# Working out the scales of staged expert weights only in slots behind a measuring pass

## The chip, the core and the metric

The kernel runs on one core of a Trainium2 chip: TensorE (PE) multiplies matrices, VectorE (DVE), ScalarE (ACT) and GpSimd (POOL) work elementwise, SyncE (SP) issues most transfers, and 16 DMA engines move the data. The metric is the time of one execution on the device, in microseconds (us); lower is better.

## What is computed

The reference is an attention layer whose output goes through a layer of experts. The attention part (a pooled softmax attention plus a narrow local one over 8 batches, 8 heads, 576 positions, 64 wide) is not touched. Behind it each of 4608 rows goes to one of eight experts:

```python
N, D, E, F = (4608, 512, 8, 1024)
expert_idx = np.argmax(logits, axis=1)
gate_w = probs[np.arange(N), expert_idx]
for e in range(E):
    mask = expert_idx == e
    h = np.maximum(x[mask] @ w1[e], 0.0)
    out[mask] = gate_w[mask, None] * (h @ w2[e])
```

## The kernel before

The attention comes first (about 350 us). Its rows are sorted into **slots** of 128 rows that share an expert. Three slots run early; then `run_slots` runs 38 more, b = 0 to 37, each as one pass of a loop that is written out in full. The slots stand in the order of their experts, so the expert changes in seven of the 38.

Products are made exact enough by splitting each operand into two float16 halves: a high one and a remainder. A slot is therefore two blocks of 24 matmuls: **mm1** (`x @ w1`, lines 1079 to 1081) and **mm2** (lines 1104 to 1106). A pass runs mm1 of its own slot and then mm2 of the slot before, so that the relu and its transposes have time. The rows x and the hidden rows h are turned by DMA transposes (tiles `xT`, line 1033, made two passes ahead; `hT`, line 1092).

An expert's weights come from HBM as float32 into a staging tile (`st`, one for w1, one for w2), 2 MB each. Before they are split they are scaled by a power of two that follows from the sum of squares of the whole matrix. That takes three steps, spread over passes:

- `measure` (lines 897 and 752): one ScalarE pass over the staged matrix, which leaves partial sums of squares in `wsq`;
- `rescale` (line 891): `total` adds them over the partitions with a tiny matmul on TensorE (line 760, columns for w1 and w2) and VectorE takes its result (line 761); `scales` makes `winv` and `wscl` in three more VectorE instructions (lines 768 and 770);
- `split_all` (lines 776 and 777): ScalarE and VectorE write the two halves of the new expert's weights. `stage_next` then issues the load of the next expert's matrix on SP, which takes place only if a flag says so.

What a pass does with the weights is decided on the chip by a **code** for each slot: 0 nothing, 1 measure w1, 2 measure w2, 3 to 5 a new expert (split; with 4 or 5 measure on the spot). `flags` loads it into a register of ScalarE, VectorE and GpSimd two slots ahead, and `renew` branches on it with `tc.If`: `renew(0, b + 1)` for w1 behind mm1, `renew(1, b)` for w2 behind mm2. Measuring comes in the second and third slot behind a new one, so the codes run: new, 0, 1, 2, then 0 until the next new one. `rescale` has no branch: it runs in 37 passes, whatever the code.

The order of work on each engine is the order in which the code is written (a manual schedule). In a pass: `flags(b + 2)`, mm1, its relu, `rescale`, `renew(0, b + 1)`, `stage_next(0, ...)`, gathers and norms, `x_split(q + 2)`, mm2 of the slot before, its output, `renew(1, b)`, `stage_next(1, ...)`, gate and store. An engine that passes an untaken `tc.If` takes an event instead, which waits until the engine's own earlier work is finished and then adds what the body would have added to the engine's count.

Of the kernel before, what the change touches and what calls it, by code (L numbers as in the profile page):

```python
# [15 lines left out]
ET = mybir.EngineType  # L16
# [32 lines left out]
class Kern:  # L49
# [834 lines left out]

    def flags(self, b):
        nc, f = self.nc, self.flg[:1, b, :]
        code = nc.values_load(f[:, 2:3], engines=(ET.Activation, ET.DVE, ET.Pool), min_val=0, max_val=5)
        self.ft[b] = [code, nc.sync.value_load(f[:, 0:1], min_val=0, max_val=1),
                      nc.sync.value_load(f[:, 1:2], min_val=0, max_val=E - 1)]

    def rescale(self):

        self.total(slice(0, 2))
        self.scales(slice(0, 2))

    def measure(self, which):
        self.square(self.st[which], which, None)
# [36 lines left out]
    def run_slots(self, q0, q1):  # L934

        last = q1 - 1
        for q in range(q0, q1):
            b = q - NEARLY
            if b + 2 < q1 - NEARLY:
                self.flags(b + 2)  # L940
            self.mm1(q)
            if not b:
                self.mm2_part(q - 1, 6, ps=self.begun)
            if q < last:
                self.rescale()
                self.renew(0, b + 1)
                self.stage_next(0, b + 1)
            if not b:
                self.out_rows(q - 1, self.begun)
                self.store(q - 1)  # L950
            if q + 4 < q1:
                self.gather(q + 4)
            if q < last:
                self.norms(q + 1)
            if q + 2 < q1:
                self.x_size(q + 2)
            self.logits(q)
            if q + 2 < q1:
                self.x_split(q + 2)
            if q > q0:  # L960
                ps = self.mm2_part(q - 1)
                if q < last:
                    self.out_rows(q - 1, ps)
            if q > q0:
                self.renew(1, b)
                if q == last:
                    self.out_rows(q - 1, ps)
                self.stage_next(1, b)
            self.gate(q)
            if q > q0:  # L970
                self.store(q - 1)
            self.scale_gate(q)
        self.mm2(last)
        self.store(last)
# [7 lines left out]
    def last_slots(self):  # L982

        q0, q1 = NEARLY + NFIX, NEARLY + NSLOT
        more = self.nc.values_load(self.flg[:1, NFIX, 3:4], min_val=0, max_val=1)  # L985
        with self.tc.If(more > 0):
            for q in range(q0, min(q0 + 4, q1)):
                self.gather(q)
            for b in (NFIX, NFIX + 1):
                self.flags(b)  # L990
            for w in range(2):
                self.renew(w, NFIX)
                self.stage_next(w, NFIX)
            self.open_slots(q0)
            self.run_slots(q0, q1)
# [125 lines left out]
    def run(self):  # L1121
# [53 lines left out]
        self.out_rows(0, ps)  # L1175
        flags = self.slot_flags()
        next(flags)
        self.hidden(2, 0, self.mm1_half(2, 0))
        for _ in range(2):
            next(w1)  # L1180
        next(flags)
        self.store(0)
        self.hidden(2, 1, self.mm1_half(2, 1))
# [59 lines left out]
```

## Time and profile before

| | us |
|---|---|
| time, median of 3 runs | 829.72 (828.9 to 831.03) |
| the profiled execution, its own time | 827.14 |
| its span in the trace | 825.4 |
| TensorE busy in the span | 732.9 (89%) |
| the stretch of the 38 slots, 382.9 to 811.6 | 428.7 |
| TensorE busy in that stretch | 404.4 |

Busy time of TensorE is the modelled length of its matmuls, which overlap: one counts 0.38 us, but the next starts 0.215 us later. So in the slots the starts are read, not the ends. "PEq" or "ACTq" stands for an engine's sequencer, which handles branches, events and register loads ("PEldq" is TensorE's).

### The profile page before, as it was taken

Reading aid. Unit: us, or ns where it says so; the run is one execution under the profiler, and the core shown is the slowest. Engines: PE = TensorE matmul, PEld = TensorE weight load, DVE = VectorE, ACT = ScalarE, POOL = GpSimd, SP = SyncE. Lnnn points to the kernel's source line nnn. Section 1 sums busy time; section 2 is a strip of 40 time slices with the busy share of each in tenths; the row PEclk is TensorE's granted clock in tenths of the full one; section 3 lists DMA queues with packets and bytes.
Section 4 is the critical chain, followed back from the end, with each engine's and each line's share of the span. In section 5 each row is a group of like instructions: output and inputs, shape, how many; then the busy total and the mean of one; then the engine's idle time right before and its main releaser. Section 6 shows DMA issues by size and latency. Waiting matters only on the chain. (4 is left out here: it accounts for less than half of the span.)

```text
span 825.4 us, 22041 instructions
## 1 busy us (share of the span) xinstructions
PE 732.9 (89%) x7460; PEld 440.6 (53%) x7460; DVE 517.5 (63%) x1571; ACT 504.1 (61%) x1095; POOL 414.8 (50%) x845
## 2 busy tenths in 40 slices
PE   7699698888797999879899989999998999998993
PEld 5487587677676777434344434444444444443441
DVE  7579598877599799773734735555463356446420
ACT  6478687777787685325654655666675347546520
POOL 6276466465557475463745344555445535544421
PEclk8889698988699889989999999999999999999997
DMA  7447856575756566764996797969598659659840
GB/s 173 114 129 169 225 122 179 135 211 131 215 134 181 137 172 222 214 140 98 199 209 133 207 180 205 220 181 228 136 278 135 142 137 259 147 117 259 140 100 21
DMA packets 246420, 138.91 MB, mean 168 GB/s; under 512 B 176626, under 2 KB 222706, under 8 KB 246272
## 3 DMA queue, kind: packets, MB, share of 16 engines
q1 hardware_dynamic: 238464, 116.05, 60.2%
q0 software_dynamic: 6560, 19.03, 8.8%
q10 hardware_dynamic: 1248, 2.11, 0.7%
q8 instruction: 61, 1.00, 0.5%
q14 instruction: 87, 0.71, 0.3%
HBM read 213.05 MB, written 20.33 MB: 283 GB/s over the span
## 5 line engine op out<-in xcount | busy, mean ns | idle before, releaser
L1079 PE MATMUL bank<-w1h,xT 128*128 128x512 f16 x328 | 126.4, 385 | 17.3 <-DMA xT<-x 16.7
L351 ACT ACTIVATE kq<-bank 64x288 f32<-64x288 f32 x256 | 109.7, 429 | 40.7 <-PE bank L347 28.3
L1104 PE MATMUL bank<-w2h,hT 128*128 128x512 f16 x328 | 126.3, 385 | 8.4 <-DMA hT<-h 8.4
L1080 PE MATMUL bank<-w1l,xT 128*128 128x512 f16 x328 | 126.0, 384 | 1.3 <-DVEq L924 1.3
L1105 PE MATMUL bank<-w2l,hT 128*128 128x512 f16 x328 | 126.3, 385 | 0.0
L1106 PE MATMUL bank<-w2h,hT 128*128 128x512 f16 x328 | 126.2, 385 | 0.0
L1081 PE MATMUL bank<-w1h,xT 128*128 128x512 f16 x328 | 126.2, 385 | 0.0
L1117 POOL DMA_INDIRECT out_dram<-o,ids x41 | 46.5, 1134 | 143.3 <-ACTq L919 110.4
L1089 DVE SCALAR_TENSOR_TENSOR h<-bank,h 128x512 f16<-128x512 f32 x82 | 55.2, 690 | 95.8 <-ACT h L1088 68.5
L1088 ACT ACTIVATE h<-bank 128x512 f16<-128x512 f32 x82 | 47.7, 594 | 98.1 <-PE bank L1081 61.6
L378 POOL TENSOR_TENSOR pool_v<-ld_v 72x256 f32<-72x256 f32 x64 | 51.1, 816 | 76.6 <-DMA ld_v<-in_v_dram 75.2
L752 ACT ACTIVATE junk<-st 128x1024 bf16<-128x1024 f32 (+1 forms) x30 | 67.6, 2252 | 5.9 <-DVE ge L669 4.8
L365 POOL TENSOR_TENSOR pool_kq<-kq 128x288 f32<-128x288 f32 x62 | 42.3, 691 | 50.8 <-ACT kq L351 45.6
L1001 POOL DMA_INDIRECT xg<-xd,ids x41 | 45.5, 1109 | 43.8 <-POOLq L925 15.6
L1079 PEld LDWEIGHTS <-xT 128*128 128x128 f16 x328 | 32.5, 99 | 59.6 <-DMA xT<-x 21.5
L477 PE MATMUL bank<-aT,vw 70*64 70x64 f32 x1152 | 46.5, 235 | 20.0 <-DMA vw<-in_v_dram 13.7
L1104 PEld LDWEIGHTS <-hT 128*128 128x128 f16 x328 | 35.0, 107 | 44.3 <-DMA hT<-h 8.8
L1049 ACT ACTIVATE lg<-lg,lmx 128x8 f32<-128x8 f32 x41 | 12.3, 301 | 72.4 <-DVE lmx L1047 72.4
L1031 DVE SCALAR_TENSOR_TENSOR x<-xg,sc,x 128x512 f16<-128x512 f32 x41 | 30.8, 751 | 40.3 <-ACT x L1028 40.2
L477 PEld LDWEIGHTS bank<-aT,vw 70*64 70x64 f32 x1152 | 41.4, 145 | 26.9 <-DMA vw<-in_v_dram 15.3
L1081 PEld LDWEIGHTS <-xT 128*128 128x128 f16 x328 | 32.4, 99 | 41.4 <-issue 3.7
L67 POOL TENSOR_SCALAR nw_t<-nw_y,nw_a 128x1 f32<-128x1 f32 x120 | 48.1, 400 | 12.1
(223 smaller groups left out, 1605.3 us busy)
## 6 DMA issues: line engine op xcount, KB each, us to landing
st<-in_moe_w_dram SPq DMA_DIRECT2D x148, 1024.0 KB
ld_k<-in_k_dram SPq DMA_DIRECT2D x64, 144.0 KB
ld_q<-in_q_dram SPq DMA_DIRECT2D x64, 144.0 KB
ld_v<-in_v_dram SPq DMA_DIRECT2D x64, 144.0 KB
xd<-xr SPq DMA_DIRECT2D x8, 1040.0 KB
vw<-in_v_dram SPq DMA_DIRECT2D x64, 122.5 KB
st<-in_moe_w_dram SPq DMA_DIRECT2D x12, 512.0 KB
vw<-in_v_dram SPq DMA_DIRECT2D x32, 67.0 KB
```

The costliest lines, as they stand in the source:

```text
L67: g.tensor_scalar(out=t, in0=y, scalar1=y, scalar2=a, op0=ALU.mult, op1=ALU.mult)
L351: nc.scalar.activation(out=kq[h * D:(h + 1) * D, w, 3 + r:3 + r + S:2], in_=ps[r * D:(r + 1) * D], func=AF.Copy)
L378: g.tensor_tensor(out=t6[:, c], in0=vr[:, :, 0:2 * D], in1=vr[:, :, 2 * D:], op=ALU.add)
L477: nc.tensor.matmul(out=ps[h * D:(h + 1) * D, (g - g0) * 64:(g - g0 + 1) * 64], lhsT=s["vw"][:, g, j + h], rhs=s["aT"][:, g, :, h], start=T ...
L752: self.nc.scalar.activation(out=junk, in_=src, func=AF.Square, accum_out=acc)
L1079: nc.tensor.matmul(out=ps, lhsT=xT[:, 0, k], rhs=self.w1h[:, k, ns], start=(k == 0), stop=False)
L1080: nc.tensor.matmul(out=ps, lhsT=xT[:, 0, k], rhs=self.w1l[:, k, ns], start=False, stop=False)
L1081: nc.tensor.matmul(out=ps, lhsT=xT[:, 1, k], rhs=self.w1h[:, k, ns], start=False, stop=(k == self.KC - 1))
L1089: nc.vector.scalar_tensor_tensor(out=h2[:, 1], in0=ps, scalar=0.0, in1=h2[:, 0], op0=ALU.max, op1=ALU.subtract)
L1104: nc.tensor.matmul(out=ps, lhsT=hh, rhs=self.w2h[:, j, :], start=(j == 0), stop=False)
L1105: nc.tensor.matmul(out=ps, lhsT=hh, rhs=self.w2l[:, j, :], start=False, stop=False)
L1106: nc.tensor.matmul(out=ps, lhsT=hl, rhs=self.w2h[:, j, :], start=False, stop=(j == self.FC - 1))
```

## The change

The code is loaded into a register of TensorE too (`flags`). `rescale_new(b)` takes the place of `rescale` in the loop: in slot 0 it is `rescale` as before, in the others `rescale` stands in two branches and runs for codes 1 and 2 only. `last_slots`, a part that only runs when more than 38 slots are needed, gets a `rescale` of its own.

```diff
     def flags(self, b):
-        code = nc.values_load(f[:, 2:3], engines=(ET.Activation, ET.DVE, ET.Pool), min_val=0, max_val=5)
+        code = nc.values_load(f[:, 2:3], engines=(ET.Activation, ET.DVE, ET.Pool, ET.PE), min_val=0, max_val=5)
...
+    def rescale_new(self, b):
+
+        if not b:
+            return self.rescale()
+        code = self.ft[b][0]
+        with self.tc.If(code > 0):
+            with self.tc.If(code < 3):
+                self.rescale()
...
             if q < last:
-                self.rescale()
+                self.rescale_new(b)
                 self.renew(0, b + 1)
...
             for b in (NFIX, NFIX + 1):
                 self.flags(b)
+            self.rescale()
             for w in range(2):
```

A branch is taken by every engine that holds the register, so TensorE now also walks through the branches of both `renew` calls, in which it has nothing to do. Line numbers behind the new function are ten higher than before (933 for 924, 928 for 919, 1091 for 1081, 1114 for 1104). TensorE's order where mm1 ends and mm2 begins, before, in slot 21 (`Activation_49`, `DMAHW7_49`, `PE_49` are the counts of ScalarE, of a DMA queue, of TensorE itself):

```order
L1080 MATMUL bank<-w1l,xT_10669 128x512
L1081 LDWEIGHTS xT_10669
L1081 MATMUL bank<-w1h,xT_10669 128x512
L760 MATMUL bank<-wsq,onesf 128x2 [waits Activation_49]
L1104 LDWEIGHTS hT [waits DMAHW7_49]
L1104 MATMUL bank<-w2h,hT 128x512 [waits Activation_49]
```

The same place now, up to the branches of `renew(0, b + 1)`, of which the first three stand here:

```order
L1091 MATMUL bank<-w1h,xT_10728 128x512
L901 COMPARE_AND_BRANCH
L902 COMPARE_AND_BRANCH
L760 MATMUL bank<-wsq,onesf 128x2 [waits Activation_49]
L902 UNCONDITIONAL_BRANCH
L902 UNCONDITIONAL_BRANCH [waits PE_49]
L901 UNCONDITIONAL_BRANCH [waits PE_49]
L933 COMPARE_AND_BRANCH
L934 COMPARE_AND_BRANCH
```

The tiny matmul stands behind two branches. In the two bodies without it an event waits for TensorE's own count (shown at the branch behind it: `[waits PE_49]`). Behind that come the branches of `renew`, and only then mm2's first weight load.

TensorE's order where mm2 ends and the next mm1 begins, before:

```order
L1106 LDWEIGHTS hT
L1106 MATMUL bank<-w2h,hT 128x512
L924 UNCONDITIONAL_BRANCH
L1079 LDWEIGHTS xT_10855 [waits DMAHW3_49]
L1079 MATMUL bank<-w1h,xT_10855 128x512 [waits Activation_49]
L1080 LDWEIGHTS xT_10855
```

Now:

```order
L1116 MATMUL bank<-w2h,hT 128x512
L928 COMPARE_AND_BRANCH
L929 COMPARE_AND_BRANCH
L929 UNCONDITIONAL_BRANCH x2
L928 UNCONDITIONAL_BRANCH x2
L1089 LDWEIGHTS xT_10917 [waits DMAHW3_49]
L887 TENSOR_LOAD flg
L1089 MATMUL bank<-w1h,xT_10917 128x512 [waits Activation_49]
```

Two branches of `renew(1, b)` come in, and behind mm1's first weight load, which waits for `xT`, the register load of the code stands ahead of mm1's first matmul.

## Rows read from the trace of the kernel before

**Rows 1.** stretches: us, busy us (count) by engine, granted clock, DMA share, GB/s

```profile
382.90:811.60 428.70, 404.42 (x1875) 185.06 (x1873) 217.63 (x664) 240.96 (x382) 200.68 (x480) 0.98 0.80 178
578.90:581.80 2.90, 2.86 (x7) 1.04 (x8) 1.86 (x6) 2.70 (x3) 2.15 (x9) 0.50 0.89 277
513.90:517.40 3.50, 1.80 (x10) 0.62 (x8) 1.65 (x2) 3.09 (x4) 1.91 (x6) 1.00 1.17 278
```

**Rows 2.** TensorE's group: count | busy us, mean ns | idle before, releaser

```profile
L760 PE MATMUL bank<-wsq,onesf 128*128 128x2 f32 x74 | 11.1, 219 | 4.0 <-ACTq L919 4.0
```

**Rows 3.** timeline (start, length in us): ordinary slot, mm1 to mm2

```profile
565.21 0.38 PE L1081 MATMUL bank<-w1h,xT 128*128 128x512 f16 x1
565.43 0.28 PE L760 MATMUL bank<-wsq,onesf 128*128 128x2 f32 x2
565.57 0.38 PE L1104 MATMUL bank<-w2h,hT 128*128 128x512 f16 x1
```

**Rows 4.** timeline: TensorE and VectorE in a slot that takes a new expert

```profile
601.01 0.38 PE L1081 MATMUL bank<-w1h,xT 128*128 128x512 f16 x1
601.89 0.39 PE L760 MATMUL bank<-wsq,onesf 128*128 128x2 f32 x2 [0.51 <-ACTq L919]
602.14 0.38 PE L1104 MATMUL bank<-w2h,hT 128*128 128x512 f16 x1
602.17 0.21 DVE L1055 TENSOR_SCALAR lsm<-lsm,sc 128x1 f32<-128x1 f32 x1 [0.16 <-DVEq L919]
```

**Rows 5.** what TensorE waited for, slots: us, times, longest

```profile
PE bank L1079 <- DMA xT<-x: 10.0, 6, 2.9
PE bank L1104 <- DMA hT<-h: 8.4, 5, 2.7
```

**Rows 6.** timeline: TensorE's matmuls that waited for a transposed matrix

```profile
410.06 0.39 PE L1079 MATMUL bank<-w1h,xT 128*128 128x512 f16 x1 [2.89 <-DMA xT<-x]
...
428.25 0.39 PE L1104 MATMUL bank<-w2h,hT 128*128 128x512 f16 x1 [0.53 <-DMA hT<-h]
...
516.08 0.39 PE L1079 MATMUL bank<-w1h,xT 128*128 128x512 f16 x1 [1.70 <-DMA xT<-x]
...
532.81 0.39 PE L1104 MATMUL bank<-w2h,hT 128*128 128x512 f16 x1 [0.77 <-DMA hT<-h]
...
578.94 0.61 PE L1104 MATMUL bank<-w2h,hT 128*128 128x512 f16 x1 [2.74 <-DMA hT<-h]
...
625.89 0.39 PE L1104 MATMUL bank<-w2h,hT 128*128 128x512 f16 x1 [2.11 <-DMA hT<-h]
...
753.88 0.39 PE L1079 MATMUL bank<-w1h,xT 128*128 128x512 f16 x1 [1.92 <-DMA xT<-x]
```

**Rows 7.** single lines: count, ns min/median/max; who waited, us, times

```profile
L924 ACTq COMPARE_BRANCH  x37: 44/44/50, 382.5 to 790.8; - x37
...
  ACT junk L1019: 2.4, 14
...
  POOL xg L1001: 17.4, 13
  DVE lg L1020: 6.9, 12
...
L752 ACT ACTIVATE junk<-st x30: 1041/1082/3617, 82.4 to 770.4; 128x1024 bf16<-128x1024 f32 x16, 128x4096 bf16<-128x4096 f32 x14
```

**Rows 8.** a matmul's start, and ScalarE's that waited for that matmul

```profile
587.92 0.38 PE L1081 MATMUL bank<-w1h,xT 128*128 128x512 f16 x1
...
588.34 0.60 ACT L1088 ACTIVATE h<-bank 128x512 f16<-128x512 f32 x1 [0.93 <-PE bank L1081]
```

**Rows 9.** register load, TensorE's branch (ns min/median/max; first, last us); its last matmul

```profile
L887 ACTq TENSOR_LOAD <-flg x37: 273/278/692, 381.0 to 777.7; - x37
...
L986 PEldq COMPARE_BRANCH  x1: 3552/3552/3552, 808.7 to 808.7; - x1
...
811.20 0.38 PE L1106 MATMUL bank<-w2h,hT 128*128 128x512 f16 x1
```

## The prediction

> **What bounds the kernel now.** I read the busy times by stretch first, then what TensorE waited for, then single slots in the timeline. In the 428.7 us of the slots TensorE counts 404.4 us of busy time at a mean granted clock of 0.98 [rows 1]; the other engines stay under 241 us. So a slot costs what its 48 matmuls and TensorE's gaps cost, and the change has to be priced at TensorE's gaps. There are three kinds. *The seam* between mm1 and mm2, where the tiny matmul of `rescale` stands: in an ordinary slot the last mm1 matmul starts at 565.21, the tiny pair at 565.43, the first mm2 matmul at 565.57 [rows 3]. The seam is 0.36 us from start to start; without the pair it would be one matmul's pace, 0.215. *The seam of a new slot* is longer, 601.01 to 602.14 [rows 4]: the tiny matmul waits for ScalarE's event at the end of the slot before. That holds 7 times, 4.0 us in all [rows 2]. *Waits for transposes*: six for `xT` (10.0 us) and five for `hT` (8.4 us) [rows 5]. The `xT` waits come at the start of mm1 one slot behind a new one; the `hT` waits at the seam one slot later. Both are ends of transfers that stand behind the loads of weights: the DMA share is near or over 1 there [rows 1].
>
> **How often.** The first branch of `renew` was decided 37 times, and 14 passes over a whole matrix ran [rows 7]. So of the 36 slots in which the new branch stands (b = 1 to 36; 37 has no `rescale`), 14 keep it and 22 skip it. The skips are the 7 new slots, the 7 behind them, and 8 more with code 0: four just ahead of a new slot, four elsewhere.
>
> **What goes.** 22 tiny pairs at 0.143 us (0.36 less 0.215): 3.1 us. The 4.0 us of waiting in new slots doesn't go with them: mm2's own first matmul waits for ScalarE's count too (the order shows `[waits Activation_49]` on it), and the split of w2 that it reads belongs to the same branch that ended late. At 602.17 VectorE's next work had just come out of its own event there [rows 4]. So mm2 could start at about 601.9 instead of 602.14: I take 0.2 us for each new slot, not 0.9. VectorE's four short instructions run beside TensorE and are worth nothing by themselves.
>
> **What comes: the stop at the seam.** In a skipped slot TensorE's event waits until all of mm1 is finished, and the branches of `renew` follow it. Nothing can be queued behind it, so mm2's first weight load, all 24 matmuls and, through them, ScalarE's output copy wait. Before, the array never ran dry here. The price isn't in the trace for TensorE, but its parts have near rows. A matmul that starts at 587.92 lets ScalarE start at 588.34: 0.42 us from start to notice [rows 8]. What such an event costs an engine that passes it and one branch is 0.17 us of idling on ScalarE (2.4 over 14) [rows 7]. With two or three branches it is 0.58 us on VectorE (6.9 over 12) and 1.34 on GpSimd (17.4 over 13) [rows 7]. So if the next slot has code 0 (one branch) the seam is at least 0.42 + 0.17 = 0.59 and at most 0.42 + 0.58 = 1.00; I take 0.76, nearer to the low end, because the branch that sends ScalarE on is 44 ns [rows 7]: net **+0.40** (0.23 to 0.64). If the next slot is new or measures (three branches), it is 0.75 to 1.76; I take 1.01, next to VectorE's row: net **+0.65** (0.4 to 1.4).
>
> By the Trainium skill, "Advanced Engine Details and Errata", section Control Flow Timing, a compare-and-branch takes about 108 ns and a plain branch 51; the rows show 44 ns for the former on ScalarE. With the page's figures (an estimate) the nets would be +0.34 and +0.60, close to mine.
>
> **What comes: a register load on TensorE** in each slot, and two branches of `renew(1, b)`. ScalarE takes 0.28 us for its own, 0.69 at most [rows 9]. TensorE's sequencer runs ahead of the array: its only branch is recorded at 808.7, while the last matmul ahead of it starts at 811.20 [rows 9]. So these are hidden behind queued matmuls, except where the queue is empty: behind the `xT` waits the load stands between the weight load that waits and the first matmul. I take **+0.35** there (0.28 to 0.69), 7 times.
>
> **What of this lies on the path.** A stop is paid only if no transfer's end comes later.
> - Four skips far from a new slot (23, 24, 30, 36): nothing waits behind them. 4 x 0.40 = +1.6.
> - Slots ahead of a new slot and the new slot itself: `xT` two passes on was made before, so its wait swallows them. But the split of w2, and with it the load that delays `hT`, starts after mm2 of the new pass. Where an `hT` wait follows, in the first five groups, lateness there remains: +0.65 - 0.2 in the first two groups, -0.2 in the next three (their slot ahead measures and keeps `rescale`): +0.3.
> - The slot behind a new one: 0.35 + 0.65 = 1.0 each, 7 times. Five times the `hT` wait follows: 0.53, about 2.2, 0.77, 2.74 and 2.11 us [rows 6], the second by difference from the total [rows 5]. It swallows all but 0.5 and 0.2: +0.7. In the last two groups no `hT` wait follows: +2.0.
>
> Sum: 1.6 + 0.3 + 0.7 + 2.0 = **+4.6 us**; the saved pairs are already in the nets.
>
> **The clock.** Four waits are followed by some 3.4 us at a granted clock of 0.5, the 1.2 GHz level, where eight matmuls start 0.43 us apart instead of 0.215: 1.7 us each. One of these stretches stands in rows 1. They follow waits of 2.11 us and more; after 1.70 and 1.92 the clock stayed at 1.00 [rows 6, 1]. Three of the four are `hT` waits (2.2, 2.74, 2.11), which come down by about 1.0 to 1.2, 1.7 and 1.1, below the longest that had no fall: -5.1. The `xT` wait of 1.70 grows by 0.2 + 0.35 to 2.25, above the shortest that had one: +1.7. Net **-3.4**, the least certain term.
>
> 4.6 - 3.4 = +1.2 us on the profiled 827.14: 828.3. The three runs' median, 829.72, lies 2.6 us above that execution, of which the kernel's waits for transfers are the natural cause; on it the forecast is **830.9**, inside 0.3% (2.5 us), about what a measurement of this kernel can tell from no change.
>
> **The rivals.**
> - *The stop is dearer* (slower). TensorE's sequencer needs for its event and branches what GpSimd's row says rather than ScalarE's: nets +0.64 and +1.4. Then the four free skips give 2.6, the last two groups 3.5, the first two 2 x 1.2, less 0.6, and the `hT` waits of 0.53 and 0.77 leave 2.2: +10.1, with the clock's -3.4 +6.7, without it +10.1: 836.4 to 839.8. It decides from nets of about 0.6 and 1.0 on, or, with my nets, if only one of the falls of the clock goes. For it: a control step was never on TensorE's path in this loop, and GpSimd loses 1.34 us where VectorE loses 0.58. Against: most of that may be GpSimd's own work ending.
> - *The clock pays for it* (faster). All four falls go and none comes, -6.8, with the nets at their low ends (+1.0, -0.1, 0.3 and 1.4, or +2.6): -4.2, 825.5. For it: the wait of 1.92 without a fall. Against: the longest wait, 2.89, keeps its length but for what two stops ahead of it take.
> - *Jumps leave the loaded code.* TensorE's one recorded branch took 3552 ns [rows 9]; it goes to the end of the program. The skips add at least two jumps to each of 22 slots; if one in eleven of these 44 cost as much, 4 x 3.55 = +14: 845. The Trainium skill says in "Runtime: NRT & Kernel Launch", Instruction fetch mechanics, that a taken branch to a target outside the loaded window has to fetch it first. Against: the new jumps pass about ten instructions, and the 37 decisions of ScalarE's branch took 50 ns at most [rows 7].
> - *It doesn't do what it says:* were the body run in all slots, the seam would stay fed and only the 0.35s remain: +0.7 after the `hT` waits' share, no change. The counts above speak against it.
>
> **How the numbers follow.** Forecast (no change to speak of) 0.45, dearer stop 0.36, clock 0.15, jumps 0.03, no effect 0.01. Of the forecast's own spread a little lies above 2.5 us and less below. Faster by over 0.3%: 0.16; within: 0.44; slower: 0.40. The forecast alone reaches from 827.5 to 833.5; the range, from 826 to 839, leaves out the jumps, the best of the clock's case and the end of the dearer one.
>
> **What would show it.** The tiny matmul's records fall by 44, from 74 to 30 in the slots [rows 2]. The seam with the next code 0 reads about 0.76, with three branches about 1.0; at 0.36 or below, no stop exists, at 1.2 and more the dearer one is right. TensorE's register load is about 0.3 us and delays mm1's first matmul only behind an `xT` wait. The `hT` waits shrink by about 1 us each and the stretches at 0.5 go from four to two. I am wrong if waits for transfers move along with TensorE instead of swallowing its stops (up to +7 more), or if the clock falls as often as before (+3.4).

## The result, and the profile after

The changed kernel takes **836.49 us** (median of 16 runs, 830.66 to 844.87), the kernel before 828.82 in 16 runs taken with it. The ratio is **1.0088** (95% interval 1.0062 to 1.0115): slower by 0.9%, about 7.3 us. Ratios here and below leave out executions more than 1.5% above the fastest of their kernel; medians are of all. The time lies inside the predicted range and outside the forecast's own reach of 827.5 to 833.5. It is the time that the rival with the dearer stop gave.

The profiled execution took 832.37 us with a span of 830.3; before it was 827.14 and 825.4. So the profile shows +4.9 of the 7.3.

The stretch of the slots after, which answers to [rows 1], and two pieces of it (columns: stretch, its length, busy us of TensorE, its weight loads, VectorE, ScalarE, GpSimd, each with a count, then granted clock, DMA share, GB/s):

```profile
385.52:815.90 430.38, 399.14 (x1831) 178.37 (x1829) 206.50 (x576) 241.24 (x382) 208.02 (x480) 0.99 0.80 177
516.50:519.90 3.40, 3.40 (x10) 1.23 (x9) 3.40 (x4) 2.32 (x3) 1.09 (x1) 0.51 0.82 163
608.70:612.10 3.40, 2.84 (x7) 0.99 (x7) 3.23 (x3) 3.25 (x4) 1.29 (x2) 0.50 0.95 198
```

TensorE has 44 records fewer (1831 for 1875), 5.3 us less of busy time and a higher mean clock, and the stretch is 1.7 us longer. The two pieces are the only stretches of the slots at 0.5, where before there were four.

TensorE's tiny matmul, which answers to [rows 2] (count | busy us, mean ns | idle before):

```profile
L760 PE MATMUL bank<-wsq,onesf 128*128 128x2 f32 x30 | 4.2, 209 | 0.0
```

30 records where 74 stood, and no waiting in front of them: the branches do what they say.

TensorE's waits in the slots, which answer to [rows 5] (who waited, for whom: us in total, times, longest):

```profile
PE bank L1114 <- ACT h L1098: 8.9, 8, 1.5
...
PE bank L1114 <- ACTq L935: 2.9, 3, 1.0
PE bank L1114 <- PEq L901: 2.8, 5, 1.0
PE bank L1089 <- DMA xT<-x: 2.3, 2, 1.6
...
PE bank L1114 <- PEq L902: 2.1, 3, 0.7
...
PE bank L1114 <- DMA hT<-h: 1.0, 1, 1.0
```

The five waits of 8.4 us for `hT` have become one of 1.0. In their place stand waits of mm2's first matmul (line 1114) for other engines and for TensorE's own sequencer. The names in these rows mislead: 22 seams are longer, and the view puts each down to whatever ended last. What fills such a seam is read from single rows. A skipped slot whose next code is 0, which answers to [rows 3]:

```profile
648.91 0.38 PE L1091 MATMUL bank<-w1h,xT 128*128 128x512 f16 x1
649.74 0.39 PE L1114 MATMUL bank<-w2h,hT 128*128 128x512 f16 x1 [0.46 <-PEq L901]
```

And TensorE's sequencer between these two (operation, count: ns min/median/max, first and last start; here one each):

```profile
L901 PEldq EVENT_SEMAPHORE  x1: 51/51/51, 649.3 to 649.3; - x1
L933 PEldq COMPARE_BRANCH  x1: 202/202/202, 649.5 to 649.5; - x1
```

The event comes 0.42 us behind the start of the last matmul, the same 0.42 that [rows 8] show for ScalarE. It takes 0.05, `renew`'s taken branch 0.20, the gaps between them the rest: 0.83 from start to start. A slot ahead of a new expert walks three branches:

```profile
670.93 0.38 PE L1091 MATMUL bank<-w1h,xT 128*128 128x512 f16 x1
672.27 0.39 PE L1114 MATMUL bank<-w2h,hT 128*128 128x512 f16 x1 [0.96 <-ACTq L935]
```

```profile
L933 PEldq COMPARE_BRANCH  x1: 70/70/70, 671.5 to 671.5; - x1
L934 PEldq COMPARE_BRANCH  x2: 70/123/176, 671.6 to 672.0; - x2
L935 PEldq COMPARE_BRANCH  x1: 217/217/217, 671.8 to 671.8; - x1
```

The seam is 1.34. The row names ScalarE's line 935, yet TensorE's own records fill it: two branches passed at 0.07, then 0.22 and 0.18, with about 0.06 behind each. A new slot, which answers to [rows 4], and the slot behind it:

```profile
682.42 0.38 PE L1091 MATMUL bank<-w1h,xT 128*128 128x512 f16 x1
683.50 0.39 PE L1114 MATMUL bank<-w2h,hT 128*128 128x512 f16 x1 [0.70 <-PEq L902]
...
694.79 0.38 PE L1091 MATMUL bank<-w1h,xT 128*128 128x512 f16 x1
696.27 0.39 PE L1114 MATMUL bank<-w2h,hT 128*128 128x512 f16 x1 [1.10 <-ACT h L1098]
```

1.08 in the new slot, 1.48 behind it. In a slot that measures, the old order and its 0.36 are left. TensorE's register load, which answers to [rows 9], has a median like that of the others; the longest took 1.29 us:

```profile
L887 PEldq TENSOR_LOAD <-flg x37: 297/312/1292, 375.8 to 775.3; - x37
```

Behind a wait for `xT` no queued matmul hides this load. In slot 12 the weight load starts when `xT` has come, and mm1's first matmul 0.57 us later, when the register load is over:

```profile
514.78 0.10 PEld L1089 LDWEIGHTS <-xT 128*128 128x128 f16 x1 [2.30 <-DMA xT<-x]
515.35 0.38 PE L1089 MATMUL bank<-w1h,xT 128*128 128x512 f16 x1 [2.37 <-ACT w2h L776]
```

```profile
L887 PEldq TENSOR_LOAD <-flg x1: 551/551/551, 514.8 to 514.8; - x1
```

Before, the two started together in the same slot (516.08 for the matmul in [rows 6]):

```profile
516.08 0.10 PEld L1079 LDWEIGHTS <-xT 128*128 128x128 f16 x1 [2.20 <-DMA xT<-x]
```

This profile has five such places (slots 8, 12, 16, 20 and 27), 0.32 to 0.87 us each and 3.0 in all; each is the load's own length and 0.02 more, whatever releaser the matmul's row names.

**Where the time went.** I added up, over the slots, how much longer each stretch between TensorE's starts is than at its full pace of 0.216. "Seams" are the 22 of skipped slots; "transfers" are the starts of mm1 and the seams of the other slots, which wait mostly for `xT` and `hT`; "clock" is what the blocks of 24 matmuls take above 4.96 (a wait of 1.3 for a split in slot 1 included, in both); the last column runs from slot 1's mm1 to slot 37's.

| profile | slot 1 starts | seams | transfers | clock | slots 1 to 37 |
|---|---|---|---|---|---|
| before | 383.60 | 9.1 | 22.5 | 8.0 | 412.3 |
| after | 386.25 | 22.4 | 14.2 | 4.7 | 414.1 |

Seams +13.4, transfers -8.3, clock -3.3: +1.8. The transfers after contain the 3.0 us of register loads and 1.7 of two starts that wait for ScalarE (slots 5 and 22), so the waits for `xT` and `hT` themselves fell by some 13. Another 2.65 us stand ahead of slot 1, where no changed step is seen to be late, and 0.4 behind slot 37. So this one execution shows the stops and most of what swallowed them. Whether transfers always swallow that much is what the experiments had to tell.

### The profile page after: what moved, and what is told of

It reads as the page before. It is cut to its first block, busy times and chain, and to the rows that moved or that the text cites. A ratio compares the mean times of both kernels' runs of the same rounds, so it can differ in the third digit from the quotient of the medians.

```text
span 830.3 us, 22402 instructions
## 1 busy us (share of the span) xinstructions
PE 728.5 (88%) x7416; PEld 437.5 (53%) x7416; DVE 500.6 (60%) x1483; ACT 505.9 (61%) x1095; POOL 421.9 (51%) x845
## 5 line engine op out<-in xcount | busy, mean ns | idle before, releaser
L1114 PE MATMUL bank<-w2h,hT 128*128 128x512 f16 x328 | 124.5, 380 | 19.9 <-ACT h L1098 8.9
L1116 PE MATMUL bank<-w2h,hT 128*128 128x512 f16 x328 | 124.3, 379 | 0.0
L1115 PE MATMUL bank<-w2l,hT 128*128 128x512 f16 x328 | 124.3, 379 | 0.0
L1127 POOL DMA_INDIRECT out_dram<-o,ids x41 | 45.2, 1104 | 131.1 <-ACTq L928 96.0
L1114 PEld LDWEIGHTS <-hT 128*128 128x128 f16 x328 | 33.1, 101 | 65.0 <-issue 29.6
L477 PE MATMUL bank<-aT,vw 70*64 70x64 f32 x1152 | 44.1, 227 | 21.8 <-DMA vw<-in_v_dram 17.0
L1089 PEld LDWEIGHTS <-xT 128*128 128x128 f16 x328 | 32.6, 99 | 53.7 <-DMA xT<-x 14.7
L67 POOL TENSOR_SCALAR nw_t<-nw_y,nw_a 128x1 f32<-128x1 f32 x120 | 51.3, 427 | 12.1
L1090 PEld LDWEIGHTS <-xT 128*128 128x128 f16 x328 | 32.6, 99 | 44.0 <-issue 7.9
L1091 PEld LDWEIGHTS <-xT 128*128 128x128 f16 x328 | 32.6, 99 | 41.8 <-issue 4.8
```

Source lines behind the costliest of these rows:

```text
L67: g.tensor_scalar(out=t, in0=y, scalar1=y, scalar2=a, op0=ALU.mult, op1=ALU.mult)
L1089: nc.tensor.matmul(out=ps, lhsT=xT[:, 0, k], rhs=self.w1h[:, k, ns], start=(k == 0), stop=False)
L1090: nc.tensor.matmul(out=ps, lhsT=xT[:, 0, k], rhs=self.w1l[:, k, ns], start=False, stop=False)
L1091: nc.tensor.matmul(out=ps, lhsT=xT[:, 1, k], rhs=self.w1h[:, k, ns], start=False, stop=(k == self.KC - 1))
L1114: nc.tensor.matmul(out=ps, lhsT=hh, rhs=self.w2h[:, j, :], start=(j == 0), stop=False)
L1115: nc.tensor.matmul(out=ps, lhsT=hh, rhs=self.w2l[:, j, :], start=False, stop=False)
```

## Experiments

All ratios are to the kernel before, run beside them, with 95% intervals.

| run | median us | ratio |
|---|---|---|
| e1, a register of its own | 836.59 | 1.0059 (1.0018 to 1.0100) |
| e2, TensorE walks, no branch on rescale | 828.95 | 0.9985 (0.9944 to 1.0026) |
| e3, VectorE's part in branches, the pair in every slot | 825.96 | 0.9970 (0.9939 to 1.0001) |
| e4, rescale in slot 0 only | 824.20 | 0.9938 (0.9897 to 0.9980) |
| e5, before without loads | 800.44 | 0.9674 (0.9637 to 0.9710) |
| e6, the change without loads | 817.15 | 0.9857 (0.9819 to 0.9894) |
| e7, the sum on GpSimd | 981.23 | 1.1860 (1.1807 to 1.1913) |
| e8, the change again | 841.12 | one execution |
| e9, second register load alone | 833.03 | 1.0060 (1.0016 to 1.0104) |
| e10, e1 without loads | 808.36 | 0.9756 (0.9697 to 0.9815) |
| e11, rescale behind mm2 | 829.38 | 1.0038 (0.9996 to 1.0080) |
| e12, e11 with VectorE's part in branches | 831.34 | 1.0023 (0.9981 to 1.0066) |

In the last four the kernel before itself spread from 819.75 to 840.0 (median of all its 29 runs 830.78); by the medians of all runs e9 is at 1.003, e11 at 0.998, e12 at 1.001.

**e1: the event without the walk.** TensorE and VectorE get the code a second time, into a register of their own, and only `rescale_new` branches on it; `renew`'s register is not on TensorE.

```diff
+        self.own[b] = nc.values_load(f[:, 2:3], engines=(ET.DVE, ET.PE), min_val=0, max_val=5)
...
-        code = self.ft[b][0]
+        code = self.own[b]
```

> The changed kernel, but TensorE and VectorE load the code into a register of their own, which only the two branches of the rescale use; the branches of the weights are walked by ScalarE, VectorE and GpSimd alone, as before. Theory 'stop' (TensorE's wait for its own mm1 at the seam, and the branches that follow it, make the loss): the stop stays in 22 seams but nothing is walked behind it, so a skipped seam reads 0.6 to 0.75 us from start to start in ordinary slots, whatever the next code, where the changed kernel has 0.83 and 1.3 to 1.5; the time lies between, ratio 1.001 to 1.005. Theory 'walk' (TensorE's way through the branches of the weights is the loss, also where mm2 ends): ratio 0.998 to 1.002. Theory 'elsewhere' (transfers, clock, the attention stage): 1.009 as measured for the change.

A skipped seam, the last mm1 matmul and the first of mm2, and TensorE's sequencer there:

```profile
660.73 0.38 PE L1093 MATMUL bank<-w1h,xT 128*128 128x512 f16 x1
661.26 0.38 PE L1116 MATMUL bank<-w2h,hT 128*128 128x512 f16 x1
```

```profile
L903 PEldq EVENT_SEMAPHORE  x1: 51/51/51, 661.1 to 661.1; - x1
```

0.53, below the 0.6 to 0.75 that I expected: the event alone costs 0.17 more than the seam with the pair. The branches behind it make the other 0.30 of the 0.83, and 0.81 of the 1.34. All 22 seams together are 9.7 us here, 0.6 more than before. Yet the kernel is slower by 0.6%, which its seams don't explain, and its interval overlaps that of the change: that the walk is the larger part is read from the seams and not from the times. e9 and e10 take the loss up.

**e2: the walk without the event.** The register is on TensorE, which walks through `renew`; `rescale` stays in every slot.

```diff
-        code = nc.values_load(f[:, 2:3], engines=(ET.Activation, ET.DVE, ET.Pool), min_val=0, max_val=5)
+        code = nc.values_load(f[:, 2:3], engines=(ET.Activation, ET.DVE, ET.Pool, ET.PE), min_val=0, max_val=5)
```

> The kernel before, with the code loaded on TensorE too: TensorE walks through all branches of the weights, in which it has no work, and the rescale runs in every slot as before. Theory 'stop': no event of TensorE's own is in these branches, so its queue stays fed; seams read 0.36, new slots 1.1 to 1.4; only the register load behind the waits for xT can show, 0.3 us a time; ratio 1.000 to 1.003. Theory 'walk': ratio 1.005 to 1.010, with seams well above 0.36.

No loss that can be measured, and the seams stay at 0.36. The same branches cost nothing where no event holds them until the array is dry: the sequencer walks them while queued matmuls run. Only the register load is not hidden here either, behind seven waits for `xT` (4.3 us in the profile), and the time doesn't show it. So the price of the change is event and walk together.

**e3: VectorE's part alone in branches.** `total` (the pair and VectorE's taking of it) in every slot, `scales` in the two branches, nothing on TensorE.

```diff
+        self.total(slice(0, 2))
         with self.tc.If(code > 0):
             with self.tc.If(code < 3):
-                self.rescale()
+                self.scales(slice(0, 2))
```

> The changed kernel without TensorE's part in it: the tiny matmul and its copy by VectorE run in every slot as before, and only the three instructions that make the scales stand in the branch, which ScalarE, VectorE and GpSimd take with the register that they had. Theory 'stop': seams read 0.36 again, ratio 0.998 to 1.002. If VectorE's branch and event in 22 slots were the loss (they delay the splits and with them the transfers): 1.004 and more.

The loss is gone; of the kernels that load all weights only e4 has a lower median, but the interval touches 1. The seams are 0.36, those of new slots as long as before (7.1 us over pace in seven, before 6.9).

**e4: no rescale behind slot 0.** Later experts are scaled by the first one's power of two.

```diff
             if q < last:
-                self.rescale()
+                if not b:
+                    self.rescale()
```

> The kernel before with the rescale in slot 0 alone, so that all later experts are scaled with the first one's power of two: what the change could have saved at most. Ordinary seams read 0.215 instead of 0.36, 36 times 0.143 = 5.1 us of TensorE's time. If new slots wait for ScalarE's event on mm2's own account, as predicted, their seams stay at 0.8 to 1.2 instead of 0.215. Ratio 0.993 to 0.997; if the waits for transfers swallow most of it, 0.997 to 1.000.

Here the seam of a new slot, which was 1.13 in [rows 4], is 0.37:

```profile
604.18 0.67 ACT L1114 ACTIVATE o<-bank,gt 128x512 f32<-128x512 f32 x1
...
604.58 0.38 PE L1082 MATMUL bank<-w1h,xT 128*128 128x512 f16 x1
604.95 0.38 PE L1105 MATMUL bank<-w2h,hT 128*128 128x512 f16 x1
```

mm2 starts 0.10 us behind ScalarE's output copy. All 22 seams are 1.0 us over pace, 8.0 less than before, while the waits for transfers are 28.9, 6.4 more: most of what the seams gave the transfers took back in that profile. The gain in the time is 0.6%, 5 us.

**e5 and e6: without the loads of later experts.** `stage_next` issues nothing, in the kernel before and in the changed one. The transposes then have the DMA engines for themselves.

```diff
     def stage_next(self, which, b):
...
-        for i in range(2):
-            self.stage(which, bass.ds(nxt, 1), i, cond=cond)
+        return
```

> The kernel before without the loads of the next experts' weights (stage_next issues nothing, so later experts are computed with weights that were staged earlier; the splits and measuring passes still run). No 2 MB loads stand in the queues, so the waits for xT and hT and the half-rate stretches behind them should go: 30.4 us of them stand in the profile of the kernel before (11.4 at mm1's start, 11.0 at seams of measuring slots, 8.0 of half rate). Seams stay at 0.36 and 1.1 to 1.4. Expected 795 to 808 us, ratio 0.960 to 0.975. It is the base for the next run.

> The changed kernel without the same loads. Theory 'swallowed' (transfers hide a part of the stops): with nothing to hide them, the whole growth of the seams shows, 13.4 us as summed from the changed kernel's profile (22.4 us over the pace in skipped and new slots, 9.1 before), so this kernel is 11 to 14 us slower than the one without loads before. Theory 'all paid' (the measured 7.3 us are all that the stops cost, nothing was hidden): 6 to 8 us slower. If transfers moved along with TensorE and grew: under 6.

TensorE's waits in the slots of e5:

```profile
PE bank L760 <- ACTq L917: 3.8, 7, 0.9
PE bank L1078 <- DVEq L922: 1.3, 1, 1.3
```

No wait for a transfer is left, and the kernel is 27 to 29 us faster. In e6 (first rows):

```profile
PE bank L1112 <- ACT h L1096: 9.9, 10, 1.3
PE bank L1112 <- ACTq L933: 2.9, 3, 1.0
PE bank L1112 <- PEq L899: 2.8, 5, 1.0
```

The stops stand there bare: 22 seams at 22.0 us over pace, in e5 8.8. The change costs 16.7 us here (817.15 less 800.44; 15 by the two ratios) and 7.3 with the loads. That is more than the 11 to 14 of the first theory. In the two profiled executions, whose spans differ by 21.6, 13.2 are seams, 6.0 lie ahead of slot 1, and 1.7 are a stretch at a granted clock of 0.50 in slot 1. So with the loads 8 to 9 us less of the change is seen, which speaks for waits and clock hiding stops. How much of it is hidden stop isn't shown, since what lies ahead of slot 1 is none. The forecast had 8.6 of 9.8 hidden.

**e7: the sum over partitions on GpSimd.** The pair goes; `partition_all_reduce` and the maximum run on GpSimd inside the branches.

```diff
-                self.rescale()
+                g.partition_all_reduce(self.wmx[:, c], self.wsq[:, c], channels=128, reduce_op=bass.bass_isa.ReduceOp.add)
+                g.tensor_scalar(out=self.wmx[:, c], in0=self.wmx[:, c], scalar1=1e-36, scalar2=None, op0=ALU.max)
+                self.scales(c)
```

> The changed kernel, but behind a measuring pass GpSimd adds the partial sums over the partitions, so TensorE has no part in the rescale (but in slot 0), needs no register and walks no branch. Theory 'stop': ordinary seams 0.215, no stop, ratio 0.993 to 0.997, like the rescale done once. Rival: GpSimd's addition holds up its gathers, stores and norms in 14 slots, and through the gate ScalarE's output copy; then 0.998 to 1.005.

GpSimd around one of the 14 sums:

```profile
574.63 0.20 POOL L1079 TENSOR_TENSOR gt<-gt,wout 128x1 f32<-128x1 f32 x1
580.85 0.41 POOL L903 PARTITION_ALL_REDUCE wmx<-wsq  x1 [6.03 <-issue]
588.40 0.24 POOL L904 TENSOR_SCALAR wmx<-wmx 128x2 f32<-128x2 f32 x1 [7.14 <-issue]
```

```profile
L903 POOLq MODIFY_POOL_CONFIG  x28: 24/25/34, 425.8 to 922.5; - x28
```

The sum itself is 0.41 us, but GpSimd does no work for 6.0 us ahead of it and for 7.1 behind it, and for about as long at each of the others. Two `MODIFY_POOL_CONFIG` instructions stand at each sum (28 for 14 in the view of its line), and two more at the line behind. That is 14 times 13 us, 182 in all, on the engine that gathers and stores the rows; the kernel takes 152 us longer, where I had expected 1.005 at most. What GpSimd does in the standstill no record shows.

**e8: the change once more**, unaltered, to see another execution.

> The changed kernel once more, for a second profile. The stops are a matter of the program: 22 seams as in the first, 0.83 with one branch behind, 1.3 to 1.5 with three, 1.07 in new slots, each within 0.1. The waits for xT and hT and the half-rate stretches are not: their sum, 18.9 us in the first profile and 30.4 before, may lie anywhere between 15 and 35. If instead the stops vary as the waits do, the sum of seams is no term to build on.

Its seams sum to those of the first profile within 0.3 us (22.7 for 22.4); two new slots are 0.2 longer each. Its transfers are 21.2 (3.6 of them register loads, behind seven waits) and its clock 6.5, so slots 1 to 37 take 423.2 us, 10.9 more than before: seams +13.6, transfers -1.3, clock -1.5. The stops are nearly the same in both executions; what swallows them isn't. A long wait needn't bring a fall of the clock either: behind this one in slot 16 the granted clock stayed at 1.00 (the columns of the stretch as in the result):

```profile
566.70 0.38 PE L1089 MATMUL bank<-w1h,xT 128*128 128x512 f16 x1 [2.72 <-DMA xT<-x]
```

```profile
566.50:570.00 3.50, 3.30 (x16) 1.53 (x16) 3.50 (x4) 3.25 (x4) 1.09 (x1) 1.00 0.90 209
```

**e9 and e10: where e1's loss comes from.** e9 is the kernel before with e1's second register load and no branch on it. e10 is e1 without loads of weights.

```diff
+        self.own[b] = nc.values_load(f[:, 2:3], engines=(ET.DVE, ET.PE), min_val=0, max_val=5)
```

> The kernel before with the second register load (VectorE and TensorE, the code two slots ahead) and nothing else of the variant with a register of its own: no branch on it, the scales worked out in every slot. If that variant's loss of about 5 us (ratio 1.006) comes from the load itself (about 0.3 us on each of the two engines in 36 slots, on the way to the transposes of x and h), the ratio here is 1.004 to 1.006. If the loss was the stop of TensorE at its seam, which in that variant was only 0.17 us dearer than in the kernel before, or the ends of the transfers moving by chance, the ratio is 1.000 to 1.002 and the seams read 0.36.

> The variant with a register of its own (rescale in two branches, no walk of TensorE through renew), without the loads of later experts' weights, which leaves out the weights of all experts but the first. No wait for a transfer is left to hide anything. If a stop without branches behind it costs what its seams show, 22 of them at 0.17 more than the seam with the tiny pair, the time is the 800.4 of the kernel before without loads plus 3 to 4 us (803.5 to 804.5), against 817.2 with the change. If the walk through renew's branches behind the event is not what makes the stop dear, it is near 817.

e9 turned out to try VectorE's load alone. Nothing on TensorE reads the register there, and its trace has an event of 51 ns on TensorE where e1 has the load (VectorE's row beside it):

```profile
L889 PEldq EVENT_SEMAPHORE  x42: 51/51/51, 376.4 to 781.6; - x42
L889 DVEq TENSOR_LOAD <-flg x37: 298/302/329, 386.4 to 788.9; - x37
```

e9 keeps the old seams and its ratio is that of e1, though by the medians of all runs it is 1.003. One row of its waits, which answers to a wait of 1.32 of the kernel before for the split of w1 in slot 1:

```profile
PE bank L1082 <- DVEq L926: 2.7, 1, 2.7
```

e10 shows the same place from VectorE's side, where its second half of the relu starts:

```profile
388.73 0.38 PE L1089 MATMUL bank<-w1h,xT 128*128 128x512 f16 x1 [0.44 <-ACTq L933]
...
389.83 1.29 DVE L1099 SCALAR_TENSOR_TENSOR h<-bank,h 128x512 f16<-128x512 f32 x2 [2.79 <-ACT o L1123]
...
391.78 0.59 PE L1090 MATMUL bank<-w1l,xT 128*128 128x512 f16 x1 [2.67 <-DVEq L933]
```

In e5 VectorE starts this step 0.25 us ahead of mm1's first matmul (382.28 and 382.53), here 1.10 behind it. The second load stands ahead of it on VectorE, so slot 1's second matmul waits 1.35 us longer, and a stretch at half rate follows, 1.7 us: 3.0 us in one place, as much as e1's own profile shows there. e1's profile also has 3.2 us of TensorE's register load behind its waits for `xT`; how much of that reaches its time isn't shown. e10 takes about 8 us more than e5, where I had expected 3 to 4, though its seams are only 0.9 longer in all; in the two profiled executions, whose spans differ by 11.8, 3.0 lie in slot 1 and 6.2 ahead of it. Its time lies about halfway to e6's +16.7, so neither expectation came. That the stop is cheap without the walk is shown by the seams (+0.9, in e6 +13.2), not by this time.

**e11 and e12: the pair away from the seam.** `rescale` in every slot, moved behind mm2 and ahead of `renew(1, b)`; e12 has `scales` in branches as in e3.

```diff
             if q < last:
-                self.rescale()
+                if not b:
+                    self.rescale()
                 self.renew(0, b + 1)
...
             if q > q0:
+                if q < last:
+                    self.rescale()
                 self.renew(1, b)
```

> The kernel before with rescale in every slot, moved from the seam to behind mm2, ahead of renew(1, b); no branch is added. If the seam of a new slot was long only because the tiny pair waits there for ScalarE's event and holds ScalarE's output copy up with it, the seams of new slots fall from 1.1 to about 0.35 and the others to 0.215, while the pair costs its 0.14 at the other seam, mm2 to mm1: 5 to 6 us of TensorE's time are free, of which the waits for transfers take some: ratio 0.994 to 0.998. If the wait moves along (the pair behind mm2 then waits for the split that ends late), the ratio is 1.000 or above.

> As the one with rescale behind mm2, and VectorE's three instructions that make the scales in branches for codes 1 and 2 (TensorE's pair in every slot, no branch on TensorE). If VectorE's short instructions count only through what stands behind them, the ratio is that of the kernel with rescale behind mm2 within 0.002; if they delay the transposes of the next slots, it is 0.003 lower.

The waits of e11 (first rows):

```profile
PE bank L1107 <- DMA hT<-h: 13.7, 5, 3.7
PE bank L1082 <- DMA xT<-x: 4.9, 4, 1.8
PE bank L760 <- ACT w1h L776: 4.3, 7, 0.7
```

The seams fall to 0.22, new slots too. But seven waits of the pair, 4.3 us, turn up again at its new place, now for the split of w1, and `hT` waits for 13.7 us where it was 8.4. No gain can be measured, and the gain I expected of e11 (0.994 to 0.998) didn't come; what I had named for a wait that moves along did. e12 is 0.0015 below e11; with intervals of some 0.004 to either side that doesn't part its two cases.

## Why the prediction came out as it did

The bound was named rightly: the time went where TensorE stands at its seams. The price of the stop was too low, and what hides it varies. By steps:

- **What goes** (22 pairs): right, 44 records fewer. **New slots**, -0.2 each: measured -0.12 (6.9 to 6.05 us over pace in seven). The reason given was wrong. I took mm2 to be held by ScalarE's late event with or without the pair; e4 and e11 show 0.35 and 0.22 there without it. The pair and VectorE's taking of its result were together the cause (no run parts these two), and the change doesn't gain it only because it puts a stop of 1.08 in their place.
- **The stop with one branch**, net +0.40: measured +0.48 over four (0.83 to 0.88). Its first part, 0.42 from the last start to the event, was exact. The rest is 0.41 where I had 0.34.
- **The stop with three branches**, net +0.65: measured +0.98 ahead of a new slot and about +1.19 behind one. This is the term that failed. I took VectorE's row (0.58) for what event and branches cost, and ScalarE's branch of 44 ns in it. TensorE takes 0.07 for a branch that it falls through and 0.18 to 0.22 for one that it takes (the row of 670.93), with some 0.06 behind each. Summed over 22 seams: forecast +7.35 (4 x 0.40, 11 x 0.65, less 7 x 0.2), measured +13.4. The rival's nets were 0.64 and 1.4, above both.
- By the Trainium skill, "Advanced Engine Details and Errata", section Control Flow Timing, a compare-and-branch takes about 108 ns. On TensorE the records show 65 to 76 ns passed and 0.2 to 0.36 us taken, so the one figure lies between and is too low for the way that decided here.
- **What swallows the stops.** The forecast let the waits take 5.2 of 9.8 us (7.35 and 7 x 0.35) and the clock 3.4 more. The profile after agrees with it better than the time: transfers -8.3, clock -3.3, two half-rate stretches for four, as said. In part that is luck: the stretch of slot 12 I had named, but the other stands in slot 20, where I had none, while the wait of 2.89 that I kept is gone. The lengths of waits from which I took falls of the clock don't hold in e8 (2.72 without a fall), which has -1.3 and -1.5 for transfers and clock. e5 and e6 set the measure: 15 to 17 us without the loads, 7.3 with them. "Waits for transfers move along with TensorE", which I had named as the way to be wrong, is in part what happens; that `hT` is made from mm1's own result fits it, but no run here tried that by itself.
- **The register load** at +0.35 behind `xT` waits: the place was right, the size too small, 0.32 to 0.87 with a mean of 0.6 in five places (3.0 us for my 2.45). Of loads without stops I had expected +0.7 us on the path, a ratio of 1.001; e2's interval, up to 1.0026, holds that and can't tell more.
- **VectorE's four instructions** "are worth nothing by themselves": for three of them e3 leaves that open (0.9939 to 1.0001); for the fourth, the taking of the pair's result, it was wrong in new slots, as above.
- **Jumps that leave loaded code:** none is seen; the longest of TensorE's branches in the slots is 0.36 us, not 3.55.

Sum by the runs: seams +13.4 in the profile, of which transfers and clock take back 11.6 there and 2.8 in e8 (both against the one profile of the kernel before), and +7.3 is what the times show, with whatever of it lies ahead of slot 1. The forecast and its rival differed in the price of the three-branch stop; the price was 1.5 to 1.8 times what I took, and the cover was as large as hoped in one execution and a quarter of that in the other. That the time is the rival's is in part luck: its nets were too high, 19.0 us of growth with the register loads (2.6 + 15.4 - 1.4 + 2.45) where 16.4 are measured (13.4 + 3.0).

What stays open: slot 1 starts at 385.8 to 388.7 in all six profiles with register loads of the code on TensorE and at 382.5 to 384.0 in six of the eight others; e9 (387.1) and e11 (387.8) are late without these loads. The lateness is there before the first of them (already in the matmuls of line 597, 350.5 for 348.0). e2 has it in its profile, an execution of 837.25 us, but no loss in its median of 828.95. Whether it belongs to the change or to chance these runs don't tell; 2.65 of the 4.9 us between the two profiled spans are this.

## What to carry to other kernels

A branch around a tiny instruction on the engine that sets the pace is dear for the event in the path not taken: that event waits for the engine's own last result, and every branch queued behind it is then paid in full. Here the event alone cost 0.17 us more than the instruction, and the branches behind it 0.30 to 0.81. Ahead of it the same branches were free. Before work is skipped on such an engine, price the dry stop (last start to notice, plus each branch) against the instruction saved, here 0.6 to 1.3 us above the pace against 0.14; if other engines do most of the work, branch there and leave the tiny instruction in place (e3: no loss, though no gain is shown either).

## What the runs showed of the hardware

- TensorE's compare-and-branch took 65 to 76 ns passed and 0.2 to 0.36 us taken; the same instruction 34 to 56 ns on ScalarE, VectorE and GpSimd:

```profile
L901 PEldq COMPARE_BRANCH  x36: 65/70/345, 389.0 to 790.7; - x36
L901 ACTq COMPARE_BRANCH  x36: 39/44/50, 393.1 to 794.8; - x36
L901 POOLq COMPARE_BRANCH  x36: 34/40/45, 393.7 to 790.4; - x36
L901 DVEq COMPARE_BRANCH  x36: 43/50/56, 393.7 to 795.4; - x36
```

- A stop of TensorE until its own last matmul is finished: 0.53 us from start to start with nothing behind it (e1), 0.31 above the pace.
- A register load on TensorE that stands behind a weight load that waits held up the next matmul by 0.32 to 0.87 us in the changed kernel; it was hidden where matmuls were queued.
- Around one sum over partitions of 0.41 us GpSimd did no other work for some 13 us, each of 14 times (e7); `MODIFY_POOL_CONFIG` instructions stand on both sides, and that they are the reason isn't shown.
- Of the 22 stops 19 repeat to within 0.07 us from one execution to the other, the rest to within 0.22; the waits for transfers and the clock's half-rate stretches of the same kernel differ by 7 us and more (14.2 and 21.2 us in the two executions of the change).
